# First and fourth output block turned together; a batch's logits turned between two heads' values; the running sum on GpSimd

## The chip, the cores and the metric

The kernel runs on one core of one Trainium2 chip. The metric is the device time of one execution in microseconds (us); of a kernel the median of several executions is given. The engines of the core are TensorE (PE, whose weight loads the profile lists apart as PEld), VectorE (DVE), ScalarE (ACT), GpSimd (POOL) and SyncE (SP, which issues the DMAs).

## What is computed

Causal attention with a decay, and behind it a soft mixture of experts over the attention's output. All data are fp32.

```python
# attention: q, k, v (8, 8, 576, 64), f (8, 8, 576)
scores = scale * q @ k.T + cum[:, None] - cum[None, :]     # cum = cumsum(log(clip(f)))
attn = softmax(where(causal, -1e9, scores)) ; out = attn @ v
x = out.transpose(0, 2, 1, 3).reshape(4608, 512)
# soft mixture: phi (512, 32), w1 (8, 512, 1024), w2 (8, 1024, 512)
logits = x @ phi                                            # (4608, 32)
slot_input = softmax(logits, axis=0).T @ x                  # over all tokens
slot_out[e] = relu(slot_input[e] @ w1[e]) @ w2[e]
result = softmax(logits, axis=1) @ slot_out
```

The softmax over all tokens is built batch by batch: each batch brings its maximum and its sum, and a running sum (`lrun`) and a running result (`acc`) are scaled by the change of the maximum.

## The kernel before

A main loop runs over g = 1 to 31, the pairs of heads (4 pairs make a batch of 576 tokens). The instructions of every engine stand in the order in which the program text issues them; no planner moves them, and each waits for what it reads. The stage of pair g does, on PE: the score tiles of its two heads (`s2`, lines 283 and 284: a matmul for q and k and one for what rounding left), between them the top pass of later heads (`s1`, line 230, whose row maxima `tops` takes on DVE, lines 244 and 246), the turnings of the pair before (`px`, line 342: one 128x128 block of X is transposed into PSUM; block t of five) and at the stage's end the values (`s3`, line 315: 50 products of probabilities and V, 100 matmuls in the trace, of 64 columns each; 60 of them complete the first head). Behind the values ACT's exponentials (`expo`, line 290), DVE's `norm` (lines 330, 331, 335: output divided by its sum, written to X), ACT's copies of turned blocks (`xcopy`, lines 372, 375, 377), ACT's roundings of q and k to the matmul's short format (`round_k`, `round_q`, lines 183 and 188) and GpSimd's subtractions of the rounded from the whole (`low_k`, `low_q`, lines 209 and 214) and its causal masks (lines 298, 301) run beside PE.

The batch's part of the mixture is spread over the stages that follow it. With b the batch that is complete and w = (g - 4) mod 4: w = 0, at the end: `logits` (line 389); w = 1: `weigh` (copies of the logits to LG), `mgroup`, `mtop`, `mcast` (the maximum, brought to all partitions as `mb`), then `weigh2` (line 431: exponential EX of the logits with its sum read out; line 432: GpSimd copies EX[0:32, 128:192] to EX[0:32, 192:256]; line 437: the factor of the maximum), `total` (line 446: `lrun` on ACT), and at the stage's end `tokens(b, 0, 1)` (lines 456, 457, 459: EX in two blocks and LG are transposed into one PSUM tile `tk`; the block of line 457 is the one with the copy; line 464: ACT copies the first part to LD); w = 2: `combine(b, 0)` (lines 495, 496: DVE reads the other part of `tk`) and `dispatch` (line 475). There are 7 batches in the loop; the eighth is done behind it.

PSUM: `scratch` tiles (pool `ps_s`) form a ring of three, used by `s1`, by logits, `tk` and dispatch's result; `turn()` gives score tiles and the small results of `mcast` from another ring of three; `pv` holds the two heads' values and, in the free columns and after `norm`, the turned blocks.

The part of a stage that the change touches, from line 738 on, is in this order: s2(h0, 0); norm of the last pair's second head; with w = 2 combine(b, 0); s1(u0, 2); s2(h0, 1); s1(u0, 3); px(g - 1, 0); s2(h0, 2); px(g - 1, 3); s1(u0, 0, 1). At the end: round_k of both heads; with w = 1 weigh2 and total; round_q of both heads; thirty products of the values; norm(h0); twenty products; with w = 1 tokens.

Of the kernel before, what the change touches and what calls it, by code (L numbers as in the profile page):

```python
# [9 lines left out]
AF = mybir.ActivationFunctionType  # L10
ALU = mybir.AluOpType
# [9 lines left out]
NG = B * NPAIR  # L21
# [54 lines left out]
def attn_softmoe(ctx: ExitStack, tc: tile.TileContext, qk, v, f, phi, w1, w2, cst, out):  # L76
    nc = tc.nc
# [102 lines left out]
    def round_k(g, *hs):  # L180
        if pair(g):
            for h in hs or range(2):
                nc.scalar.copy(WA[g % 3][0:64, S * h : S * h + S], RAW[g % 3][64:128, h])  # L183

    def round_q(g, *hs):
        if pair(g):
            for h in hs or range(2):
                nc.scalar.copy(YA[g % 3][0:64, h, 64:640], RAW[g % 3][0:64, h])  # L188
# [133 lines left out]
    def norm(i):  # L322
        if not head(i):
            return
        g, h = divmod(i, 2)
        b, p = divmod(g, NPAIR)
        x, o = xtile(b, p // 2), pvv[h]
        at = 128 * (p % 2) + 64 * h
        rl = small.tile([P, NBLK], F32, name=f"rl{i}", tag="rl")
        nc.vector.tensor_scalar_add(rl, o[:, :, 64], EPS)  # L330
        nc.vector.reciprocal(rl, rl)
        rl = rl.rearrange("p (t o) -> p t o", o=1)
        for ts in (slice(0, NBLK),) if i < NH - 1 else (slice(0, NBLK, 4), slice(1, 4)):
            to = x[:, ts, at : at + 64]
            nc.vector.tensor_tensor(to, o[:, ts, 0:64], rl[:, ts].broadcast_to(list(to.shape)), op=ALU.mult)  # L335
# [24 lines left out]
    def px(g, t):  # L360
        if pair(g):
            n, o = TURN[t]
            turned(pv[n][:, o : o + 128], g, t)
# [62 lines left out]
    def weigh2(b):  # L426
        if not batch(b):
            return
        mb = st["mb", b]
        if b < B - 1:  # L430
            nc.scalar.activation(EX[:, 0:192], LG[:, 0:192], AF.Exp, bias=mb[:, 1:2], accum_out=mb[:, 2:3])
            nc.gpsimd.tensor_copy(EX[0:32, 192:256], EX[0:32, 128:192])
        else:
            nc.scalar.activation(EX[:, 0:192], st["lg", b][:, 0:192], AF.Exp, bias=mb[:, 1:2])
            nc.vector.tensor_copy(EX[0:32, 192:256], EX[0:32, 128:192])
        if b > 0:
            nc.scalar.activation(mb[:, 3:4], st["mb", b - 1][:, 1:2], AF.Exp, bias=mb[:, 1:2], scale=-1.0)

    def total(b):
        if not batch(b):  # L440
            return
        mb = st["mb", b]
        if b == 0:
            nc.scalar.copy(lrun, mb[:, 2:3])
        elif b < B - 1:
            nc.scalar.activation(lrun, lrun, AF.Identity, scale=mb[:, 3:4], bias=mb[:, 2:3])
        else:
            nc.vector.scalar_tensor_tensor(lrun, in0=lrun, scalar=mb[:, 3:4], in1=mb[:, 2:3], op0=ALU.mult, op1=ALU.add)

# [36 lines left out]
    def combine(b, step):  # L486

        if not batch(b):
            return
        ce = ctok[:, b]  # L490
        if step == 0:

            lt = st["tok", b][:, 224:384].rearrange("p (t s) -> p t s", t=NBLK)
            sm = st["sm", b] = const.tile([P, 2, NBLK], F32, name=f"sm{b}", tag="sm", bufs=1)
            nc.vector.tensor_reduce(sm[:, 0], lt, axis=AX.X, op=ALU.max)
            nc.vector.tensor_tensor(ce, lt, wide(sm[:, 0]), op=ALU.subtract)
        elif step == 1:
            st["ce"] = turn()
            nc.scalar.activation(st["ce"][:, 0 : NBLK * NS].rearrange("p (t s) -> p t s", t=NBLK), ce, AF.Exp)
        else:  # L500
            sm, pm = st["sm", b], st["ce"]
            et, to = pm[:, 0 : NBLK * NS].rearrange("p (t s) -> p t s", t=NBLK), pm[:, NBLK * NS : NBLK * NS + NBLK]
            nc.vector.tensor_reduce(to, et, axis=AX.X, op=ALU.add)
            nc.vector.tensor_scalar_add(sm[:, 1], to, EPS)
            nc.vector.reciprocal(sm[:, 1], sm[:, 1])
            nc.vector.tensor_tensor(ce, et, wide(sm[:, 1]), op=ALU.mult)
# [218 lines left out]
    for g in range(1, NG):  # L725
        h0, h1 = 2 * g, 2 * g + 1
        u0, u1 = h0 + 3, h0 + 4
        b, w = divmod(g - 4, NPAIR)
        c = b - 1 if w == 0 else b if (b, w) == (B - 2, 3) else None
        if g < 4:  # L730
            load_v(g + 1)
            load_qk(g + 3)
        else:
            load_qk(g + 3)
            load_v(g + 1)
        if w == 1:
            weigh(b)
        low_q(h0 + 2)
        low_q(h1 + 2)
        s2(h0, 0)  # L740
        expo(h0, 0)
        norm(h0 - 1)
        if w == 1:
            mgroup(b)
        if w == 2:
            combine(b, 0)
        s1(u0, 2)
        tops(u0, 2)
        s2(h0, 1)
        expo(h0, 1)  # L750
        s1(u0, 3)
        tops(u0, 3)
        if 1 < g < NG - 1:
            px(g - 1, 0)
        s2(h0, 2)
        expo(h0, 2)
        if g == NG - 1:
            px(g - 1, 0)
        if g > 1:
            px(g - 1, 3)  # L760
        else:
            round_k(3, 0)
            round_q(3, 0)
        s1(u0, 0, 1)
        tops(u0, 0, 1)
        if g > 1:
            px(g - 1, 1)
        s2(h0, 3)
        if g > 1:
            xcopy(g - 1, (0, 3))  # L770
            px(g - 1, 2)
            xcopy(g - 1, (1, 2))
        s2(h0, 4)
        s1(u0, 4, 5)
        s2(h0, 5)
        expo(h0, 3)
        tops(u0, 4, 5)
        causal(h0)
        low_k(h0 + 2)
        if w == 1:  # L780
            mtop(b)
        s2(h1, 0)
        expo(h1, 0)
        if g == 1:
            for t in (0, 3, 1, 2):
                px(0, t)
        px(g - 1, 4)
        if g == 1:
            xcopy(0, (0, 3))
            xcopy(0, (1, 2))  # L790
        if g == 1:
            xcopy(0, (4,))
        s1(u1, 2)
        tops(u1, 2)
        s2(h1, 1)
        expo(h1, 1)
        s1(u1, 3)
        tops(u1, 3)
        s2(h1, 2)
        mturn(g + 1)  # L800
        mrows(g + 1)
        expo(h1, 2)
        if g > 1:
            xcopy(g - 1, (4,))
        s1(u1, 0, 1)
        tops(u1, 0, 1)
        s2(h1, 3, 4)
        s1(u1, 4, 5)
        s2(h1, 5)
        expo(h1, 3)  # L810
        tops(u1, 4, 5)
        causal(h1)
        low_k(h1 + 2)
        if g == 1:
            round_k(3, 1)
            round_q(3, 1)
        load_cum(g + 3)
        dup_q(g + 2)
        dup_k(g + 2)
        if 2 <= g < NRES + 2:  # L820
            wload(g - 2)
        if g == 29:
            sides[2].close()
            p2 = fresh(ctx, "p2", 2)
            wstream(*p2, RAW[30 % 3])
        if g == 30:
            sides[1].close()
            xp = ctx.enter_context(tc.tile_pool(name="xp", bufs=1))
            X.append(xp.tile([P, NBLK, 256], F32, name="X3"))
            p0 = fresh(ctx, "p0", 1)  # L830
            p1 = fresh(late, "p1", 3)
            wstream(*p0, *p1, RAW[31 % 3])
        if g == 31:
            sides[0].close()
            with tc.using_default_side("right"):
                tp = ctx.enter_context(tc.tile_pool(name="tp", bufs=1))
            cT = tp.tile([P, sum(CUT)], F32R, name="cT")
            wstream(tp.tile([P, QW], F32, name="w36"))
        if w == 1:
            mcast(b)  # L840
        if c is not None:
            combine(c, 1)
        if w == 2 and b < B - 2:
            dispatch(b, *range(NBLK))
        if g == NG - 1:
            st["lg", B - 1] = scratch(False, f"lg{B - 1}")
            nc.vector.memset(st["lg", B - 1][:, 128:192], -1.0e30)
        round_k(g + 3)
        if w == 1:
            weigh2(b)  # L850
            total(b)
        round_q(g + 3)
        if c is not None:
            combine(c, 2)
        s3(g, VALUES[:30])
        norm(h0)
        if g == 31:
            logits(B - 1, 0, 1)
            wstream(XTS[:, 0:QW], PTS[:, 0:QW])
            split(0, 0)  # L860
            split(1, 0)
        s3(g, VALUES[30:])
        if w == 0:
            logits(b, *range(NPAIR))
        if w == 1:
            tokens(b, 0, 1)
        if g == 28:
            wstream(RAW[29 % 3])
    logits(B - 1, 2)
# [3 lines left out]
    b = B - 1  # L873
# [267 lines left out]
```

## Time and profile before

| | |
|---|---|
| median of 3 executions | 390.61 us (390.54 to 391.75) |
| the profiled execution | 390.4 us, its span 388.7 us |
| PE busy | 370.2 us, 95% of the span |
| PEld busy | 329.6 us |
| DVE busy | 280.8 us |
| ACT busy | 275.3 us |
| GpSimd busy | 254.8 us |
| values (line 315), PE | 102.0 us, 3200 matmuls |
| turnings (line 342), PE | 42.1 us, 155 matmuls |
| low_k and low_q, GpSimd | 180.0 us, 128 instructions |

The profile is of one execution, and times within it count from the start of its span. Matmuls overlap each other, so the distance from one start (or one end) to the next is what a matmul costs, not its duration.

### The profile page before, as it was taken

The page shows a single profiled execution, that of the slowest core. Times are in us where ns is not written, and L with a number is a line of the kernel's source. Part 1 is how long each engine was busy: PE and PEld are TensorE (multiplying, and loading weights), DVE is VectorE, ACT ScalarE, POOL GpSimd, SP SyncE. Part 2 cuts the span into 40 slices and gives each one's busy share as a digit, 9 for nine tenths or more (in the row PEclk, how much of TensorE's full clock was granted, in tenths as well). Part 3 has the DMA queues.
Part 4 walks back from the last instruction along what each step waited for, and adds up shares of the span by engine and source line. Part 5 has one row for each costly group of instructions (what it writes and reads, how often), then busy time and mean ns, then how long its engine had stood idle before and what let it go on. Part 6 is the DMA issues. An engine that isn't in the chain of part 4 may idle for free.

```text
span 388.7 us, 15148 instructions
## 1 busy us (share of the span) xinstructions
PE 370.2 (95%) x5863; PEld 329.6 (85%) x5863; DVE 280.8 (72%) x1079; ACT 275.3 (71%) x670; POOL 254.8 (66%) x357
## 2 busy tenths in 40 slices
PE   8999999999999999999999999999999998999870
PEld 7889999999999999999999999999999985567640
DVE  7878887878887888788878887888788535441680
ACT  8969887878787878787878887878787653021560
POOL 4988887878787878787878787878787821000000
PEclk9999999999999999999999999999999999999995
DMA  6875878777777777777777777777777899996798
GB/s 206 207 196 161 251 227 242 216 213 212 216 211 215 217 212 214 214 215 212 213 214 216 213 214 214 214 214 216 212 215 209 264 334 362 417 417 257 264 390 321
DMA packets 34344, 93.72 MB, mean 241 GB/s; under 512 B 4266, under 2 KB 8288, under 8 KB 34272
## 3 DMA queue, kind: packets, MB, share of 16 engines
q1 hardware_dynamic: 34272, 92.75, 76.7%
q8 instruction: 46, 0.75, 0.8%
q14 instruction: 26, 0.21, 0.2%
HBM read 63.93 MB, written 9.73 MB: 190 GB/s over the span
## 4 chain that ended last, share of the span: by engine, by line
PE 90%; DMA 3%; DVE 3%; issue 1%; ACT 1%; DVEq 0%; ACTq 0%
PE pv L315 26%; PE ring L283 15%; PE s L230 13%; PE ring L284 13%; PE pv L342 5%; PE pv L981 4%; PE more L941 4%; PE lg L389 3%; DMA out<-RAW 3%; PE ds L475 2%; DMA PTS<-in_f 1%; PE ring L511 1%; PE pv L256 1%; PE ring L1058 1%; PE tk L456 0%
## 5 line engine op out<-in xcount | busy, mean ns | idle before, releaser
L290 ACT ACTIVATE PTS<-ring 128x320 f32<-128x320 f32 (+2 forms) x256 | 119.9, 501 | 42.3 <-PE ring L284 33.5
L283 PE MATMUL ring<-YA,WA 67*128 67x320 f32 (+9 forms) x384 | 121.3, 329 | 0.0
L246 DVE CUSTOM_DVE_ANT_0 s<-s,mask 128x320 f32<-128x320 f32 (+3 forms) x256 | 109.2, 442 | 5.2 <-PE s L230 0.6
L284 PE MATMUL ring<-YB,WB 128*128 128x320 f32 (+4 forms) x384 | 110.4, 295 | 0.0
L315 PE MATMUL pv<-V,PTS 128*64 128x65 f32 x3200 | 102.0, 223 | 0.0
L315 PEld LDWEIGHTS pv<-V,PTS 128*64 128x64 f32 x3200 | 97.0, 138 | 2.9 <-issue 1.6
L230 PE MATMUL s<-WA,YA 66*128 66x288 f32 (+9 forms) x384 | 97.6, 310 | 0.8 <-ACT YA L188 0.4
L209 POOL TENSOR_TENSOR WB<-RAW,WB 64x576 fp32r<-64x576 f32 x64 | 90.4, 1413 | 10.6 <-ACT WA L570 4.8
L214 POOL TENSOR_TENSOR YB<-RAW,YA 64x576 fp32r<-64x576 f32 x64 | 89.6, 1421 | 2.6 <-POOL EX L397 0.2
L283 PEld LDWEIGHTS ring<-YA,WA 67*128 67x128 f32 (+3 forms) x384 | 69.7, 183 | 5.5 <-issue 2.1
L284 PEld LDWEIGHTS ring<-YB,WB 128*128 128x128 f32 (+1 forms) x384 | 69.9, 182 | 0.0
L230 PEld LDWEIGHTS s<-WA,YA 66*128 66x128 f32 (+1 forms) x384 | 62.8, 190 | 7.5 <-ACT PTS L290 1.6
L301 POOL TENSOR_SCALAR_AFFINE_SELECT PTS<-PTS 128x128 f32<-128x128 f32 (+1 forms) x128 | 31.5, 267 | 22.1 <-ACT PTS L290 20.6
L246 DVE DVE_READ_ACCUMULATOR2_ANT MT<- 128x1 fp32r x310 | 43.9, 142 | 0.0
L298 POOL TENSOR_SCALAR_AFFINE_SELECT PTS<-PTS 128x384 f32<-128x384 f32 x64 | 33.5, 523 | 13.4 <-ACT PTS L290 9.4
L342 PE MATMUL pv<-cs,X 128*128 128x128 f32 x155 | 42.1, 278 | 0.1
L183 ACT CAST WA<-RAW 64x576 fp32r<-64x576 f32 x64 | 40.2, 669 | 2.6 <-DMA RAW<-in_qk 1.8
L188 ACT CAST YA<-RAW 64x576 fp32r<-64x576 f32 x64 | 40.3, 670 | 0.4
L246 DVE CUSTOM_DVE_ANT_0 s<-s,mask,MT 128x288 f32<-128x288 f32 x62 | 32.6, 526 | 10.0 <-PE s L230 1.4
L330 DVE TENSOR_SCALAR rl<-pv 128x5 f32<-128x5 f32 x64 | 10.5, 164 | 35.1 <-PE pv L315 24.8
L335 DVE TENSOR_TENSOR X<-pv,rl 128x320 f32<-128x320 f32 (+1 forms) x65 | 31.5, 486 | 2.4 <-DMA V<-in_v 0.3
L244 DVE TENSOR_REDUCE MT<-s 128x1 fp32r<-128x288 f32 x62 | 27.9, 450 | 0.0
(220 smaller groups left out, 386.5 us busy)
## 6 DMA issues: line engine op xcount, KB each, us to landing
w<-in_w SPq DMA_DIRECT2D x45, 512.0 KB
RAW<-in_qk SPq DMA_DIRECT2D x31, 576.0 KB
V<-in_v SPq DMA_DIRECT2D x32, 325.0 KB
YB<-YA SPq DMA_DIRECT2D x30, 288.0 KB
WB<-WA SPq DMA_DIRECT2D x30, 288.0 KB
p<-in_w SPq DMA_DIRECT2D x6, 512.0 KB
out<-RAW SPq DMA_DIRECT2D x6, 512.0 KB
out<-p SPq DMA_DIRECT2D x5, 512.0 KB
```

The lines of the kernel that those rows point to most:

```text
L183: nc.scalar.copy(WA[g % 3][0:64, S * h : S * h + S], RAW[g % 3][64:128, h])
L188: nc.scalar.copy(YA[g % 3][0:64, h, 64:640], RAW[g % 3][0:64, h])
L209: nc.gpsimd.tensor_tensor(t[0:64], RAW[g % 3][64:128, h], t[64:128].bitcast(F32), op=ALU.subtract)
L214: nc.gpsimd.tensor_tensor(YB[g % 2][64:128, h], RAW[g % 3][0:64, h], YA[g % 3][0:64, h, 64:640].bitcast(F32), op=ALU.subtract)
L230: nc.tensor.matmul(t[:, o : o + w], ya[0:m, h, 128 * blk : 128 * blk + 128], wa[0:m, j0 : j0 + w], start=True, stop=True)
L246: nc.vector.tensor_tensor_reduce(out=t[:, o : o + w], in0=t[:, o : o + w], in1=mask[:, m0 : m0 + w], scale=1.0, scalar=top.bitcast(F32) if ...
L283: nc.tensor.matmul(o, wa[0:m, j0 : j0 + n], ya[0:m, h, 64 + i0 : 64 + i0 + w], start=True, stop=False)
L284: nc.tensor.matmul(o, wb[:, j0 : j0 + n], yb[:, h, i0 : i0 + w], start=False, stop=True)
L290: nc.scalar.activation(PT[i % 2][:, SEG_O[bank] : SEG_O[bank] + at], t[:, 0:at], AF.Exp, scale=0.125)
L298: nc.gpsimd.affine_select(d3, d3, pattern=[[0, 3], [1, 128]], compare_op=ALU.is_ge, fill=0.0, base=0, channel_multiplier=-1)
L315: nc.tensor.matmul(pvv[h][64 * u : 64 * u + 64, t, :], PT[h][:, at : at + 64], V[:, g % 2, c, 65 * h : 65 * h + 65], start=(c == 0), stop= ...
L342: nc.tensor.transpose(pm[:, 0:128], x[:, t, 128 * (p % 2) : 128 * (p % 2) + 128], ident)
```

## The change

The turning px(g - 1, 0) moves behind s2(h0, 2), next to px(g - 1, 3). In stages with w = 1, tokens(b, 0, 1) moves from the end of the stage to the place between the values' thirty and twenty products, behind norm(h0) in the text; combine(b, 0) comes directly behind it, from the next stage; the second half of round_k and round_q come behind both. The copy of line 432 goes from GpSimd to VectorE, the running sum of line 446 from ScalarE to GpSimd.

```diff
--- before.py
+++ after.py
@@ -429,7 +429,7 @@
         mb = st["mb", b]
         if b < B - 1:
             nc.scalar.activation(EX[:, 0:192], LG[:, 0:192], AF.Exp, bias=mb[:, 1:2], accum_out=mb[:, 2:3])
-            nc.gpsimd.tensor_copy(EX[0:32, 192:256], EX[0:32, 128:192])
+            nc.vector.tensor_copy(EX[0:32, 192:256], EX[0:32, 128:192])
         else:
             nc.scalar.activation(EX[:, 0:192], st["lg", b][:, 0:192], AF.Exp, bias=mb[:, 1:2])
             nc.vector.tensor_copy(EX[0:32, 192:256], EX[0:32, 128:192])
@@ -443,7 +443,7 @@
         if b == 0:
             nc.scalar.copy(lrun, mb[:, 2:3])
         elif b < B - 1:
-            nc.scalar.activation(lrun, lrun, AF.Identity, scale=mb[:, 3:4], bias=mb[:, 2:3])
+            nc.gpsimd.tensor_scalar(lrun, lrun, mb[:, 3:4], mb[:, 2:3], op0=ALU.mult, op1=ALU.add)
         else:
             nc.vector.scalar_tensor_tensor(lrun, in0=lrun, scalar=mb[:, 3:4], in1=mb[:, 2:3], op0=ALU.mult, op1=ALU.add)
 
@@ -742,21 +742,16 @@
         norm(h0 - 1)
         if w == 1:
             mgroup(b)
-        if w == 2:
-            combine(b, 0)
         s1(u0, 2)
         tops(u0, 2)
         s2(h0, 1)
         expo(h0, 1)
         s1(u0, 3)
         tops(u0, 3)
-        if 1 < g < NG - 1:
-            px(g - 1, 0)
         s2(h0, 2)
         expo(h0, 2)
-        if g == NG - 1:
+        if g > 1:
             px(g - 1, 0)
-        if g > 1:
             px(g - 1, 3)
         else:
             round_k(3, 0)
@@ -845,15 +840,22 @@
         if g == NG - 1:
             st["lg", B - 1] = scratch(False, f"lg{B - 1}")
             nc.vector.memset(st["lg", B - 1][:, 128:192], -1.0e30)
-        round_k(g + 3)
         if w == 1:
+            round_k(g + 3, 0)
             weigh2(b)
             total(b)
-        round_q(g + 3)
+        else:
+            round_k(g + 3)
+            round_q(g + 3)
         if c is not None:
             combine(c, 2)
         s3(g, VALUES[:30])
         norm(h0)
+        if w == 1:
+            tokens(b, 0, 1)
+            combine(b, 0)
+            round_k(g + 3, 1)
+            round_q(g + 3)
         if g == 31:
             logits(B - 1, 0, 1)
             wstream(XTS[:, 0:QW], PTS[:, 0:QW])
@@ -862,8 +864,6 @@
         s3(g, VALUES[30:])
         if w == 0:
             logits(b, *range(NPAIR))
-        if w == 1:
-            tokens(b, 0, 1)
         if g == 28:
             wstream(RAW[29 % 3])
     logits(B - 1, 2)
```

## Rows read from the trace of the kernel before

**Rows 1.** The page: chain of work that ended last, by engine

```profile
PE 90%; DMA 3%; DVE 3%; issue 1%; ACT 1%; DVEq 0%; ACTq 0%
```

**Rows 2.** One stage: us, each engine's busy us (instructions), PEclk, DMA share

```profile
117.54:126.39 8.85, 8.85 (x146) 8.36 (x142) 6.47 (x26) 6.34 (x16) 6.55 (x8) 1.00 0.80 233
```

**Rows 3.** PEld's waits: what waited, for whom: us in total, times, longest

```profile
PEld pv L342 <- DVE X L335: 2.4, 14, 0.3
...
PEld s L230 <- ACT PTS L290: 1.6, 5, 0.3
```

**Rows 4.** Timeline of PE, w = 1: start us, us, engine, line

```profile
102.07 0.30 PE L230 MATMUL s<-WA,YA 66*128 66x288 f32 x1
...
102.46 0.31 PE L284 MATMUL ring<-YB,WB 128*128 128x320 f32 x1
```

**Rows 5.** Timeline of PE, the same place with w = 3

```profile
121.56 0.30 PE L230 MATMUL s<-WA,YA 97*128 97x288 f32 x1
...
122.09 0.32 PE L284 MATMUL ring<-YB,WB 128*128 128x320 f32 x1
```

**Rows 6.** Timeline of PE, five turnings in the first stage

```profile
28.57 0.71 PE L342 MATMUL pv<-cs,X 128*128 128x128 f32 x5
```

**Rows 7.** Timeline of all engines, a stage with w = 2

```profile
111.04 0.29 ACT L464 COPY LD<-tk 128x160 f32<-128x160 f32 x1
...
111.72 0.33 DVE L496 TENSOR_TENSOR ctok<-tk,sm 128x160 f32<-128x160 f32 x1
...
112.16 0.30 PEld L230 LDWEIGHTS s<-WA,YA 66*128 66x128 f32 x2 [0.32 <-ACT PTS L290]
```

**Rows 8.** Timeline of PE, end of the values with w = 1

```profile
109.31 0.75 PE L315 MATMUL pv<-V,PTS 128*64 128x65 f32 x20
110.00 0.33 PE L456 MATMUL tk<-cs,EX 128*128 128x128 f32 x1
110.18 0.33 PE L457 MATMUL tk<-cs,EX 128*128 128x128 f32 x1
...
110.67 0.37 PE L284 MATMUL ring<-YB,WB 128*128 128x448 f32 x1
```

**Rows 9.** Timeline of PE, end of the values with w = 2

```profile
119.81 0.87 PE L315 MATMUL pv<-V,PTS 128*64 128x65 f32 x24
...
120.92 0.37 PE L284 MATMUL ring<-YB,WB 128*128 128x448 f32 x1
```

**Rows 10.** Timeline of GpSimd beside the values with w = 1

```profile
108.43 1.41 POOL L209 TENSOR_TENSOR WB<-RAW,WB 64x576 fp32r<-64x576 f32 x1
109.90 0.23 POOL L432 COPY EX<-EX 32x64 f32<-32x64 f32 x1
```

**Rows 11.** Timeline of PE, last stage, logits between values

```profile
317.96 0.86 PE L389 MATMUL lg<-XTS,phis 128*32 128x128 f32 x16
318.75 0.57 PE L315 MATMUL pv<-V,PTS 128*64 128x65 f32 x12
```

**Rows 12.** Timeline of ACT beside the values with w = 1

```profile
107.57 1.24 ACT L183 CAST WA<-RAW 64x576 fp32r<-64x576 f32 x2
108.84 0.46 ACT L431 ACTIVATE EX<-LG,mb 128x192 f32<-128x192 f32 x1
109.20 0.19 ACT L431 ACTIVATION_READ_ACCUMULATOR EX<-LG,mb 128x1 f32 x1
```

**Rows 13.** Timeline of all engines, start of the program

```profile
3.02 1.05 POOL L539 MEMSET WA<- 2x1152 f32 x1
3.45 0.93 DVE L543 TENSOR_SCALAR PTS<-PTS 64x576 f32<-64x576 f32 x1
```

**Rows 14.** Timeline of DVE, a little later

```profile
6.52 0.46 DVE L557 CAST PTS<-PTS 64x576 fp32r<-64x576 f32 x1
```

**Rows 15.** Timeline of all engines, the eighth batch's tail

```profile
325.19 0.18 DVE L435 COPY EX<-EX 32x64 f32<-32x64 f32 x1 [0.49 <-ACT EX L434]
...
325.43 0.14 PEld L457 LDWEIGHTS more<-cs,EX 128*128 128x128 f32 x1
```

## The prediction

> **What bounds the kernel now.** I read the chain of work that ended last first: nine tenths of the span are TensorE (PE) [rows 1]. Next the busy time by stage: a stage of the main loop without logits or dispatch is 8.85 us long, and PE is busy for 8.85 us of it at a granted clock of 1.00 [rows 2]. PE has hardly a hole there, so an edit counts only by the holes that it closes or opens in PE's order. The waits of PE's weight loads (PEld) list the holes that there are: 14 in front of a turning (L342) that waits for X, and 5 in front of a score matmul of the top pass (L230) [rows 3]. The change touches both kinds, and opens a third place.
>
> **Holes that it closes.** (a) The first block's turning, px 0. In a stage without the wait, 0.39 us pass from the L230 ahead of it to the L284 behind it (102.07 to 102.46) [rows 4]; in one with the wait 0.53 (121.56 to 122.09) [rows 5]. Here 0.14 us of PE are lost; over the 14 stages of [rows 3], one of them with twice that, about 2.0 us. The change puts px 0 behind the score pair L283, L284, some 0.29 us later (two blocks of 320 columns), by which time X is there. Turned next to the fourth block (t = 3) it is the same work, 0.11 us, as in the one place where five turnings stand in a row ((0.71 - 0.27) / 4) [rows 6]; the move itself I cost at nothing. (b) In the stages with w = 2 the third tile of the top pass needs a PSUM buffer of the ring of three, which the turned logits (tk) hold until combine's step 0 has read them. The row names ACT, but the DVE subtraction L496 ends at 111.72 + 0.33 = 112.05, and the load comes at 112.16 after 0.32 us [rows 7]. L496 is late because tk is turned at the end of the stage before, and because LD's copy on ACT, which comes ahead of it, ran only at 111.04 [rows 7]. With tokens and combine(b, 0) in the middle of the values this reading is over before the next stage is under way. Five such waits [rows 3] of 0.31 us each: 1.5 us. Together 3.5 us.
>
> **What the cut of the values costs, apart from waiting.** tokens is three turnings. At the end of the stage they take 0.37 us: from the last value's end (109.31 + 0.75 = 110.06) to the end of the next L284 (110.67 + 0.37 = 111.04) are 0.98 us [rows 8], and 0.61 (120.68 to 121.29) where there are no tokens [rows 9]. Of that 0.07 is a wait: L457 comes at 110.18, not at 110.00 + 0.11, just after GpSimd's copy of EX ended at 109.90 + 0.23 = 110.13 [rows 8, 10]. In the middle, PE must leave the 64-column values and come back. Leaving: the first turning ends 0.27 us after the last value (110.06 to 110.33) [rows 8], against 0.11 behind another turning [rows 6]. Coming back is seen once, in the last stage, where logits stand between values: the twelve values behind them need from 318.82 (end of L389) to 319.32, 0.50 us [rows 11], against 0.36 at their usual pace of 0.03; so the first four end some 0.27 us after what stood ahead of them. The Trainium skill (TensorEngine Tiling (Array Packing), Key Properties) says that a change of tiling mode drains the engine; these rows agree, at about 0.15 us a change, and by that rule alone the cut would cost two more changes in each of 7 batches, 2.1 us.
>
> **What the cut waits for.** Sixty values go ahead of it; the other forty take 1.16 us (0.029 each [rows 8]), so in this stage the sixtieth ends at about 110.06 - 1.16 = 108.90. ACT: the first of two roundings of k that start at 107.57 ends 0.67 later at 108.24; the exponential comes then instead of at 108.84 [rows 12], and its accumulator is read out 0.55 us after its start (109.20 + 0.19 - 108.84), at 108.82. That is in time for the first turning. The second turning needs the copy of EX's last block, which is now VectorE's (DVE). That copy can start at 108.85. At that moment GpSimd is in its subtraction low_k (L209), 108.43 to 109.84 [rows 10], and the copy is fp32 from SBUF to SBUF. There is one such meeting in the trace: DVE's L543, 64x576 fp32 in SBUF, came at 3.45 while a GpSimd memset ran from 3.02 to 4.07, and took 0.93 us, until 4.38 [rows 13]; a cast of the same shape with GpSimd idle took 0.46 [rows 14]. L543 thus ended 0.31 us after the memset, about the streaming part of the 0.46: it looks as if DVE did nothing until GpSimd's instruction was over. The Trainium skill (SBUF — State Buffer, Who interferes with whom) says so: a DVE copy in a two-port mode and a GpSimd instruction shut each other out for the whole instruction, and whichever comes second waits. By it the copy waits until 109.84, as by the row.
>
> I take the row. The copy is over at 109.84 + 0.04 (0.31 us scaled from 576 to 64 columns); the load of L457 comes 0.05 later, as in the tail (325.37 to 325.43 [rows 15]), at 109.93; its matmul ends 0.33 later [rows 8], 110.26, the third turning 0.11 later, 110.37, and the first four values 0.27 after that, 110.64. Uncut they would end at 108.90 + 0.12 = 109.02. The cut costs 1.62 us, less 0.37 at the old place: 1.25 a batch, 8.75 us for 7 batches. Without a collision the copy takes 0.18 [rows 15], L457 loads at 109.09, and the same steps give 0.78, less 0.37 = 0.41 a batch, about 2.7 us in all (the last batch has no rounding ahead of its exponential and waits less). These are the two ends; I take the upper one, since the only row in which a DVE fp32 operation within SBUF arrives under a GpSimd instruction shows it.
>
> **What I cost at nothing.** The running sum leaves ACT and becomes one GpSimd operation on 128x1, while GpSimd's copy (0.23 us [rows 10]) goes: about even, ahead of two subtractions whose results are read a stage later; without that cover GpSimd would lose 0.2 us a batch. ACT now waits for tk ahead of the second rounding of k and both of q; it is then some 0.2 us later against PE than before. Behind them stands the first exponential of the next stage, and PE asks for that score buffer again only behind the matmuls of 112.16 [rows 7], 1.1 us after the block itself is written (111.04 [rows 8]). DVE's norm of the first head queues behind the held copy, about 0.8 us; X is read in the next stage, over 2 us later. SP's queue keeps its order, and what it loads next reads roundings that are a stage old.
>
> **The sum.** The profiled execution took 390.4 us, its span 388.7; the median of the runs is 390.61, 0.2 above. 390.4 - 2.0 - 1.5 + 8.75 = 395.65; I say 395.7.
>
> **Rivals.**
> 1. No collision: the copy runs beside low_k. For it: DVE and GpSimd are both busy through most of each stage without holding PE up; against it: DVE reads PSUM in what it does there, and [rows 13] shows the other case. 390.4 - 3.5 + 2.7 = 389.6: not slower. It decides if L457 loads within 0.3 us of the sixtieth value's end.
> 2. No collision and a cheap cut: the copy is in time and only the two changes of tile are paid, 14 times 0.15 less the 0.07 of waiting saved in each batch, 1.6: 390.4 - 3.5 + 1.6 = 388.5.
> 3. The holes stay: px 0 or the ring waits for something that comes as late. For it: the row of the second kind names another engine than I do [rows 3, 7]. With the collision 395.7 + 3.5 = 399.2, with half of the holes 397.4.
> 4. A partial collision, in which the two engines share the time: half of the difference, 392.7. Against it: L543 lost nearly all of the 0.62 us that it shared with the memset [rows 13].
>
> **How the numbers follow.** The forecast has 0.75, rival 1 0.11, rival 2 0.05, rival 3 0.03, rival 4 0.06. The forecast's own range is 394.2 to 397.2: coming back at 0.15 to 0.4 instead of 0.27 (0.9 us over the batches), a fifth of the removed holes (0.7). To leave out no more than 2 in 10 it reaches down to rival 4: 392.3 to 397.2. A measurement of this kernel can tell about 0.3% (1.17 us) from no change, so faster means below 389.44, slower above 391.78. Faster: rival 2 and a third of rival 1, 0.09; same: the rest of rival 1, 0.07; slower 0.84.
>
> **What would show it.** Right: in 7 stages PEld waits 0.8 to 1.0 us at L457 for DVE's copy; that copy is recorded with about 1 us instead of 0.18 and ends just behind GpSimd's L209; no waits stand in front of L342 in stages with w = 0 and 3, and none in front of L230 with w = 2; the way from one stage's values to the next is about 1 us longer from w = 1 to w = 2. Wrong: a copy of 0.2 us in the shadow of L209 (rival 1), an L209 that is lengthened instead (DVE goes first, and the price is GpSimd's), or a new wait of PE's L283 for ACT in the stages behind a cut.

## The result, and the profile after

The changed kernel takes 395.72 us (median of 5, 395.61 to 396.14), the kernel before 390.55 beside it: a ratio of 1.0125 (1.011 to 1.0139), 5.2 us slower. The forecast was 395.7.

From the page of the changed kernel: the busy time of each engine and the chain of work that ended last, by engine; below it the answer for the copy of line 432 alone: shortest, median and longest of seven copies in ns, then the starts of the first and the last in us.

```profile
span 393.9 us, 15143 instructions
PE 370.7 (94%) x5863; PEld 331.0 (84%) x5863; DVE 286.4 (73%) x1086; ACT 273.5 (69%) x664; POOL 254.6 (65%) x356
...
PE 87%; DVE 4%; ACT 3%; DMA 2%; issue 2%; ACTq 0%; DVEq 0%
...
L432 DVE COPY EX<-EX x7: 924/990/1059, 70.2 to 305.8; 32x64 f32<-32x64 f32 x7
```

PE does the same work as before (370.7 against 370.2 us busy) in a span that is 5.3 us longer. In the chain that ended last, PE's share fell from 90 to 87% [rows 1]; VectorE's rose from 3 to 4% and ScalarE's from 1 to 3%. The copy of line 432 takes 0.99 us instead of the 0.18 that the same operation takes in the tail [rows 15].

The waits of PE's weight loads in the changed kernel (what waited, for whom: us in total, times, longest):

```profile
PEld tk L457 <- DVE EX L432: 6.2, 7, 0.9
...
PEld s L230 <- ACT YA L188: 0.8, 1, 0.8
...
PEld pv L342 <- PE ring L284: 0.2, 1, 0.2
```

The 14 waits of turnings for X and the 5 waits of L230 for L290 [rows 3] are gone from the main loop. Seven waits of the second turning for VectorE's copy have come, 6.2 us in all.

One of these places by engine, from the timelines of DVE, GpSimd, PE and ACT (start us, us, engine, line; in brackets the idle time ahead; "..." stands for lines left out and for the next engine). The stage's values begin at 107.50.

```profile
109.42 0.99 DVE L432 COPY EX<-EX 32x64 f32<-32x64 f32 x1 [0.65 <-ACT EX L431]
110.34 0.14 DVE L330 TENSOR_SCALAR rl<-pv 128x5 f32<-128x5 f32 x1
...
108.96 1.40 POOL L209 TENSOR_TENSOR WB<-RAW,WB 64x576 fp32r<-64x576 f32 x1
110.47 0.34 POOL L446 TENSOR_SCALAR lrun<-lrun,mb 128x1 f32<-128x1 f32 x1
...
109.44 0.33 PE L456 MATMUL tk<-cs,EX 128*128 128x128 f32 x1
110.47 0.33 PE L457 MATMUL tk<-cs,EX 128*128 128x128 f32 x1 [0.70 <-DVE EX L432]
110.64 0.27 PE L459 MATMUL tk<-cs,LG 128*128 128x128 f32 x1
110.84 0.98 PE L315 MATMUL pv<-V,PTS 128*64 128x65 f32 x26
...
110.94 0.29 ACT L464 COPY LD<-tk 128x160 f32<-128x160 f32 x1 [1.37 <-PE tk L459]
```

The first turning is in time. The copy is taken up at 109.42, while GpSimd's low_k runs from 108.96 to 110.36; it ends at 110.41, 0.05 us behind low_k. Only then PE turns the second block, at 110.47, and the values go on at 110.84.

A stage in which no tokens are turned, the same one as in [rows 2] (columns as there):

```profile
119.02:127.72 8.70, 8.70 (x146) 8.37 (x142) 6.18 (x24) 6.35 (x16) 6.55 (x8) 1.00 0.82 237
```

It has become 0.15 us shorter, at the same granted clock. Where the 5.3 us of span come from, by the distance from one stage's first value to the next stage's:

| way | before | after | sum of the differences |
|---|---|---|---|
| w = 1 to 2, first batch | 10.30 | 11.52 | +1.2 |
| w = 1 to 2, five batches | 10.60 to 10.63 | 11.47 to 11.52 | +4.4 |
| w = 1 to 2, last batch | 8.55 | 9.58 | +1.0 |
| all others | | | -1.4 |
| span | 388.67 | 393.94 | +5.3 |

### The profile page after: what moved, and what is told of

It is laid out like the page before. It is cut to its first block, busy times and chain, and to the rows that moved or that the text cites. A ratio compares the mean times of both kernels' runs of the same rounds, so it can differ in the third digit from the quotient of the medians.

```text
span 393.9 us, 15143 instructions
## 1 busy us (share of the span) xinstructions
PE 370.7 (94%) x5863; PEld 331.0 (84%) x5863; DVE 286.4 (73%) x1086; ACT 273.5 (69%) x664; POOL 254.6 (65%) x356
## 4 chain that ended last, share of the span: by engine, by line
PE 87%; DVE 4%; ACT 3%; DMA 2%; issue 2%; ACTq 0%; DVEq 0%
PE pv L315 22%; PE ring L283 15%; PE s L230 13%; PE ring L284 13%; PE pv L342 4%; PE pv L981 4%; PE more L941 4%; PE lg L389 3%; PE ring L511 2%; DMA out<-RAW 2%; PE ds L475 2%; DVE EX L432 2%; ACT WA L183 1%; ACT EX L431 1%; PE ring L1058 1%
## 5 line engine op out<-in xcount | busy, mean ns | idle before, releaser
L290 ACT ACTIVATE PTS<-ring 128x320 f32<-128x320 f32 (+2 forms) x256 | 119.0, 500 | 40.7 <-PE ring L284 31.8
L283 PE MATMUL ring<-YA,WA 67*128 67x320 f32 (+9 forms) x384 | 119.3, 324 | 0.0
L246 DVE CUSTOM_DVE_ANT_0 s<-s,mask 128x320 f32<-128x320 f32 (+3 forms) x256 | 109.3, 444 | 5.3 <-PE s L230 0.7
L315 PE MATMUL pv<-V,PTS 128*64 128x65 f32 x3200 | 103.6, 223 | 0.0
L230 PE MATMUL s<-WA,YA 66*128 66x288 f32 (+9 forms) x384 | 97.8, 310 | 0.5 <-ACT YA L188 0.4
L283 PEld LDWEIGHTS ring<-YA,WA 67*128 67x128 f32 (+3 forms) x384 | 69.0, 181 | 6.3 <-issue 2.1
L230 PEld LDWEIGHTS s<-WA,YA 66*128 66x128 f32 (+1 forms) x384 | 62.9, 190 | 5.7 <-ACT YA L188 0.8
L246 DVE DVE_READ_ACCUMULATOR2_ANT MT<- 128x1 fp32r x310 | 43.9, 142 | 0.0
L246 DVE CUSTOM_DVE_ANT_0 s<-s,mask,MT 128x288 f32<-128x288 f32 x62 | 32.6, 526 | 10.3 <-PE s L230 1.4
L342 PE MATMUL pv<-cs,X 128*128 128x128 f32 x155 | 36.5, 272 | 0.0
```

Of the source, the lines that this page charges most:

```text
L230: nc.tensor.matmul(t[:, o : o + w], ya[0:m, h, 128 * blk : 128 * blk + 128], wa[0:m, j0 : j0 + w], start=True, stop=True)
L246: nc.vector.tensor_tensor_reduce(out=t[:, o : o + w], in0=t[:, o : o + w], in1=mask[:, m0 : m0 + w], scale=1.0, scalar=top.bitcast(F32) if ...
L283: nc.tensor.matmul(o, wa[0:m, j0 : j0 + n], ya[0:m, h, 64 + i0 : 64 + i0 + w], start=True, stop=False)
L290: nc.scalar.activation(PT[i % 2][:, SEG_O[bank] : SEG_O[bank] + at], t[:, 0:at], AF.Exp, scale=0.125)
L315: nc.tensor.matmul(pvv[h][64 * u : 64 * u + 64, t, :], PT[h][:, at : at + 64], V[:, g % 2, c, 65 * h : 65 * h + 65], start=(c == 0), stop= ...
L342: nc.tensor.transpose(pm[:, 0:128], x[:, t, 128 * (p % 2) : 128 * (p % 2) + 128], ident)
```

## Experiments

The question was whether the held copy is the cause, or the cut itself; then, what the rest of the change is worth. Each ratio is to runs of the kernel before on the same chip. The expectations count from 390.5 us for that kernel; beside e1 to e4 it took 391.11 us and beside e5 to e8 390.67, so a time is best compared by its ratio.

**The copy on ScalarE (e1_copy_act).**

```diff
# the changed kernel, weigh2
-            nc.vector.tensor_copy(EX[0:32, 192:256], EX[0:32, 128:192])
+            nc.scalar.copy(EX[0:32, 192:256], EX[0:32, 128:192])
```

> The changed kernel with one edit: the copy of EX's last block runs on ScalarE instead of VectorE. Theory (VectorE's copy is held by GpSimd's low_k): the copy takes 0.2 us right behind the exponential, the second turning waits about 0.1 us instead of 0.9, and 6 us come back: 389.7 us (389.2 to 390.3). Rival (the cut of the values itself costs the time, by leaving and coming back): nothing but the copy's own 0.2 us changes, 394.5 to 396.

Measured: 390.82 us against 391.11, a ratio of 0.999 (0.9974 to 1.0006). The copy takes 0.24 us, PE's loads wait 0.14 for it, and the way from the values' start to their going on is 2.58 us instead of 3.33. The time lies above the 389.2 to 390.3 that the theory gave; the interval of the ratio holds the theory's 389.7 / 390.5 = 0.998 and not the rival's 1.01. About 5 us come back with one line, not 6: the cut alone doesn't cost them.

**The same move on VectorE, as a reduction (e3_reduce).**

```diff
# the changed kernel, weigh2
-            nc.vector.tensor_copy(EX[0:32, 192:256], EX[0:32, 128:192])
+            nc.vector.tensor_reduce(EX[0:32, 192:256], EX[0:32, 128:192].rearrange("p (s o) -> p s o", o=1), axis=AX.X, op=ALU.max)
```

> The changed kernel; VectorE keeps the move of EX's last block and GpSimd keeps its order, but the move is written as a maximum over one element instead of a copy. Theory (only an operation that takes VectorE's second pair of ports is held): the reduction takes 0.2 us beside low_k, 389.6 us (389.1 to 390.3). Rival (any VectorE operation within SBUF is held by GpSimd): 0.9 us or more, 395.2 to 396.2.

Measured: 390.71 us, 0.999 (0.9975 to 1.0005); again above the theory's time, with its ratio (389.6 / 390.5 = 0.9977) just within the interval and the rival's 1.012 far outside. Its timelines of DVE, GpSimd and PE at the same place:

```profile
108.81 0.21 DVE L432 TENSOR_REDUCE EX<-EX 32x64 f32<-32x64 f32 x1 [0.66 <-ACT EX L431]
...
108.36 1.40 POOL L209 TENSOR_TENSOR WB<-RAW,WB 64x576 fp32r<-64x576 f32 x1
...
108.84 0.33 PE L456 MATMUL tk<-cs,EX 128*128 128x128 f32 x1
109.08 0.33 PE L457 MATMUL tk<-cs,EX 128*128 128x128 f32 x1
109.24 0.27 PE L459 MATMUL tk<-cs,LG 128*128 128x128 f32 x1
109.44 1.39 PE L315 MATMUL pv<-V,PTS 128*64 128x65 f32 x40
```

Same engine, same data, same moment within low_k, which runs from 108.36 to 109.76; but 0.21 us instead of 0.99. So not every VectorE operation within SBUF is held by GpSimd; the copy is. The Trainium skill (SBUF — State Buffer, Who interferes with whom) says that copies, casts and tensor_scalar can enter the modes that take the pair of ports shared with GpSimd, and that tensor_reduce on trn2 never contends; these two kernels agree with it: the copy took 0.99 us, the reduction 0.21.

**low_k behind the running sum (e2_lowk_later, e8_lowk_later_b).** The copy stays VectorE's; GpSimd's order is changed.

```diff
# the changed kernel, stage loop: the edit of e8; e2 has it without "or g == 29" and "if g < 29"
         causal(h1)
-        low_k(h1 + 2)
+        if w != 1 or g == 29:
+            low_k(h1 + 2)
...
             total(b)
+            if g < 29:
+                low_k(h1 + 2)
```

> The changed kernel; VectorE keeps the copy, but in stages with w = 1 GpSimd does low_k of the second head behind the running sum, which waits for ScalarE until the copy has started. In the first batch the running sum is ScalarE's, so there low_k still comes early. Theory (held by low_k): in six of seven batches the copy takes 0.2 us, in the first about 1.0; 390.5 us (389.8 to 391.3). Rival 1 (the cut itself): 395 to 396. Rival 2 (VectorE's copy is slow in the middle of the loop for another reason): copies of 1 us in all batches, 395 to 396.

Measured: 398.3 us, 1.0189 (1.0156 to 1.0222), outside of what the theory or either rival gave. The copies are as the theory had them, six of 0.18 us and one of 0.93. The time went elsewhere, in one wait of its loads:

```profile
PEld ring L284 <- POOL WB L209: 4.4, 1, 4.4
```

At g = 29 the moved low_k comes behind a weight load into the buffer that it reads. It waits 7.3 us for that DMA, PE waits for it, and the second head of the next pair gets the low part of its k from weights. So e2's time doesn't test the theory, only its copies do. e8 leaves g = 29 as it was.

> As the kernel in which low_k comes behind the running sum, but the stage g = 29 keeps its order, where that kernel put low_k behind a weight load into the buffer that it reads, so that it waited for the load and took wrong values of k. Theory: five batches without a held copy, the first and the last with one (0.8 us each over the kernel with the reduction): 391.7 us (391.2 to 392.4) where the kernel before takes 390.5. Rival (a collision is only moved): 395 to 396.

Measured: 392.01 us against 390.67, 1.0034 (1.0017 to 1.0051), as the theory had it. The line's answer and the wait in this kernel:

```profile
L432 DVE COPY EX<-EX x7: 182/183/1065, 70.2 to 301.8; 32x64 f32<-32x64 f32 x7
...
PEld tk L457 <- DVE EX L432: 1.8, 2, 0.9
```

Five copies without low_k beside them take 0.18 us, and for the two that meet it PE's loads still wait 0.9 us each. With VectorE's text unchanged, the copy's length follows GpSimd's order.

**The copy left on GpSimd (e6_copy_gpsimd).**

```diff
# the changed kernel, weigh2
-            nc.vector.tensor_copy(EX[0:32, 192:256], EX[0:32, 128:192])
+            nc.gpsimd.tensor_copy(EX[0:32, 192:256], EX[0:32, 128:192])
```

> The changed kernel with the copy of EX's last block left on GpSimd, as before. Theory (the cut needs the block while GpSimd is in low_k, whoever copies it): the copy starts only when low_k is over and takes 0.23 us, so the second turning waits 0.2 us longer than in the changed kernel: 397 us (396.5 to 397.6) where the kernel before takes 390.5. Rival (VectorE's copy alone is at fault): near the kernel with ScalarE's copy, 390 to 391.

Measured: 397.39 us, 1.0169 (1.0144 to 1.0195), as the theory had it. The wait in its profile:

```profile
PEld tk L457 <- POOL EX L432: 8.0, 7, 1.2
```

On GpSimd the copy stands behind low_k in the queue; on VectorE it is held until low_k is over. By the way from w = 1 to w = 2, moving it to VectorE saved 0.25 us a batch, and not the 1.0 that the reduction of e3, which isn't held, saves.

**The copy on VectorE alone (e7_copy_alone).**

```diff
# the kernel before, weigh2
-            nc.gpsimd.tensor_copy(EX[0:32, 192:256], EX[0:32, 128:192])
+            nc.vector.tensor_copy(EX[0:32, 192:256], EX[0:32, 128:192])
```

> The kernel before with one part of the change: the copy of EX's last block on VectorE. Theory: it is held by low_k as in the changed kernel, 0.9 to 1.05 us, but the turning comes 1.2 us later than in the cut and does not wait; the time stays within 0.5 us of the kernel before (0.5 us of old waits at the second turning go): 390.0 to 390.6. Rival (a held VectorE costs by what is queued behind it, norm): 391 to 393.

Measured: 391.5 us, 1.0022 (1.0005 to 1.004): the rival; the theory's upper end, 390.6 / 390.5, lies below the interval. Timeline of DVE, and its waits of PE's loads:

```profile
109.87 0.44 DVE L432 COPY EX<-EX 32x64 f32<-32x64 f32 x1 [1.22 <-ACT EX L431]
110.24 0.14 DVE L330 TENSOR_SCALAR rl<-pv 128x5 f32<-128x5 f32 x1
...
111.46 0.49 DVE L335 TENSOR_TENSOR X<-pv,rl 128x320 f32<-128x320 f32 x1
...
PEld pv L342 <- DVE X L335: 4.3, 21, 0.4
```

Both roundings of k stand ahead of the exponential here, so in six of seven batches the copy meets only the end of low_k and takes 0.37 to 0.45 us; here it ends at 110.31, 0.05 us behind low_k (108.85 to 110.26). No turning of tk waits for it. But both norms are behind it, the second X is written 0.40 us later than in the kernel before, and 7 more turnings wait for X (21 instead of 14 [rows 3]) with 1.9 us more of PEld's idle time. The way from w = 1 to w = 2 grows by 0.35 us in the first batch and 0.33 in the last; in the five between by 0.04 only, where the waits of L230 become shorter (0.9 us in all instead of 1.6 [rows 3]). A held VectorE costs by what is queued behind it, even where nobody waits for what it holds.

**px 0 alone (e4_px).**

```diff
# the kernel before, stage loop
-        if 1 < g < NG - 1:
-            px(g - 1, 0)
         s2(h0, 2)
         expo(h0, 2)
-        if g == NG - 1:
-            px(g - 1, 0)
         if g > 1:
+            px(g - 1, 0)
             px(g - 1, 3)
```

> The kernel before with one part of the change: the first block's turning moves behind the third score pair, next to the fourth block's. Theory: the 14 waits for X go and nothing takes their place, 388.4 us (388.1 to 388.8). Rival: PE meets another wait as late, 389.8 to 390.6.

Measured: 389.94 us against 391.11, 0.9953 (0.9934 to 0.9971). As a time alone that would be the rival's; the interval of the ratio holds the theory's 388.4 / 390.5 = 0.9946 and not the rival's 0.998 to 1.000. The span falls from 388.7 to 386.8. In its profile the waits for X in the main loop are gone and the ring waits stand as they were:

```profile
PEld s L230 <- ACT PTS L290: 1.5, 5, 0.3
```

From the L230 ahead of the pair of turnings to the second L230 behind it PE takes 0.80 us, as it did before without a wait.

**Both kinds of hole closed without the cut (e5_uncut).** From the kernel before: px as above, the running sum on GpSimd, EX's last block by the reduction, and another order of ACT's roundings with w = 1:

```diff
# the kernel before, end of a stage
-        round_k(g + 3)
         if w == 1:
+            round_k(g + 3, 0)
             weigh2(b)
             total(b)
-        round_q(g + 3)
+            round_k(g + 3, 1)
+            round_q(g + 3, 0)
+        else:
+            round_k(g + 3)
+            round_q(g + 3)
...
         if w == 1:
             tokens(b, 0, 1)
+            round_q(g + 3, 1)
```

> The kernel before with the part of the change that helped (px 0 next to px 3), the values left whole and tokens at the stage's end; the running sum on GpSimd as in the change; EX's last block moved by VectorE as a maximum over one element; of the roundings in stages with w = 1 only the last half of q comes behind tokens, so that LD's copy on ScalarE runs at once. Theory (of the change's gains both kinds of hole can be had without the cut): px 2.0 us, most of the five ring waits 1.2, the wait of the second turning 0.5: 387.0 us (386.5 to 387.8) where the kernel before takes 390.5. Rival (the ring wait needs the cut, since ScalarE has no earlier place for LD's copy): 388.0 to 388.6, as with px alone.

Measured: 387.26 us against 390.67, 0.9908 (0.9889 to 0.9927), as the theory had it: 3.4 to 3.6 us faster than the kernel before, and 8.5 faster than the changed one. Timelines of ACT and PE:

```profile
110.23 0.29 ACT L464 COPY LD<-tk 128x160 f32<-128x160 f32 x1 [0.19 <-PE tk L459]
110.42 0.67 ACT L188 CAST YA<-RAW 64x576 fp32r<-64x576 f32 x1
...
109.64 0.33 PE L456 MATMUL tk<-cs,EX 128*128 128x128 f32 x1
109.81 0.27 PE L457 MATMUL tk<-cs,EX 128*128 128x128 f32 x1
109.92 0.27 PE L459 MATMUL tk<-cs,LG 128*128 128x128 f32 x1
```

LD's copy starts at once behind the turnings, and the way from w = 1 to w = 2 is 10.24 us, where px alone has 10.60 and the cut with the reduction 10.73. tk is turned as late as before, at the stage's end, so the ring waits needed an earlier reading of tk, not an earlier tk. And against this kernel the cut with the reduction costs 0.49 us (10.73 - 10.24) in each of the five middle batches even without a collision: more than the 0.31 that it was to save.

## Why the prediction was right

- **The collision.** The term that carried it, 1.62 us a cut, is confirmed step by step. Counted from the stage's first value, the copy could start at 1.92 us and did at 1.92; L457's load was put at 3.00 and came at 2.97. It rested on a single meeting at the program's start [rows 13]; e3 and e8 show the cause, since neither a reduction at the same moment nor the same copy without low_k is held.
- **The cut without a collision.** 0.41 us a batch was forecast (rival 1). Against the uncut e5 it is 0.49 in five batches, 0.56 in the first and 0.32 in the last. The first four values behind the cut end 2.88 us after the stage's first value (e3), where the steps of the forecast give 2.87 (109.09 + 0.33 + 0.11 + 0.27, less the 106.93 at which that stage's values begin).
- **px 0.** 2.0 us were forecast; alone it gave 1.9 of span. In the changed kernel all that isn't the way from w = 1 to 2 gained only 1.4.
- **The ring waits.** All five went, as forecast; but e5 shows that the cut wasn't needed for it.
- **The sum.** That the time was met to 0.1 us is partly luck: two terms were off, against each other. The ways from w = 1 to 2 cost 6.7 us where 8.75 - 1.5 = 7.25 were put; of the difference 0.22 is in the last batch (1.03 instead of 1.25) and some 0.06 in each of the five middle ones; the rest gained 1.4 instead of 2.0. Where those 0.6 us went is known: from w = 0 to 1 each way is 0.03 us longer (7 of them), one stage each of 8.79 and 8.84 us stands among those of 8.70, and the way from g = 30 to 31 and what follows the last stage's first value are 0.07 longer each. In the stage of 8.79 us a load of L256 waits 0.17 us for VectorE's L246, in that of 8.84 us one of L283 waits 0.12 for ScalarE's L290. They are longer at the same place in e2, e3, e5 and e8 but not in e1, e4 or e6; why, stays open.
- **What was costed at nothing.** GpSimd's running sum takes 0.34 us, not about 0.23; no engine waits for it in the profile. That norm behind the held copy costs nothing holds in the changed kernel, where no turning of the main loop waits for X any more; in the kernel before the same cover isn't there, and e7 pays for it.
- **The rivals.** Rivals 1 and 2 (no collision) fall with the copy's 0.99 us, rival 4 (a partial one) with the copy's end 0.05 us behind low_k's in each of the seven batches, rival 3 with the waits that are gone. What was said against rival 4 was put too strongly: by [rows 13, 14] L543 lost 0.93 - 0.46 = 0.47 us, three quarters of the 0.62 that it shared with the memset, and not nearly all.

## What to carry to other kernels

Before an operation goes from GpSimd to VectorE, look at what GpSimd runs at the moment when it will be wanted: a VectorE fp32 copy within SBUF ended only 0.05 us behind GpSimd's 1.4 us instruction, and all that VectorE had queued behind it came later still. A reduction over one element, or ScalarE, moved the same data in 0.21 to 0.24 us. And where a buffer is released late, look first for the reader that is late: another order of ACT's roundings closed the holes that the cut was to close, without paying for the engine's two changes between 64-column and full tiles.

## What the runs showed of the hardware that was not expected

- VectorE's reduction of 32x64 elements takes 0.21 us and its copy 0.18 when GpSimd is out of the way: the form that isn't held costs 0.03 us.
- A GpSimd tensor_scalar on 128x1 elements took 0.34 us, longer than GpSimd's copy of 32x64, 0.23 [rows 10].
- In e1 and e5 the first values of the loop's first stage (g = 1) come 0.3 to 0.6 us later than in the others (32.12 and 31.89 against 31.53 to 31.64 us). A load of L230 waits 0.6 us for ACT ahead of them, though the text up to there is the same. The cause stays open.
